# Larger rows for the loads around the layer changes of a two-layer attention and mixer kernel, and weights loaded for two heads at a time

## The chip, the cores and the metric

The kernel runs on one core of one Trainium2 chip. The metric is the device time of one execution in microseconds (us). Three runs of the kernel before took 2493.18, 2493.18 and 2494.72 us, median 2493.18 us.

## What is computed

Two tokens (batch B = 2, one new position each, D = 512 columns) pass twice through the same pair of blocks, so there are two layers with the same weights and the same key and value caches:

```
x = x + attention(layernorm(x), k_cache, v_cache, wq, wo)
x = x + mixer(layernorm(x), w1, b1, w2, b2)
x = x + attention(layernorm(x), k_cache, v_cache, wq, wo)
x = x + mixer(layernorm(x), w1, b1, w2, b2)
```

The attention has 32 query heads in 8 groups; a group of 4 query heads shares one cache of 32768 keys and values of 128 float32 numbers. One (layer, token, group) is a *unit*: 16 MiB of keys and 16 MiB of values are read, 4 rows of scores come out of the keys, a softmax runs over all 32768 scores, and the values are summed with those weights. There are 2 x 2 x 8 = 32 units. The mixer takes one scalar per column through a small network (1792 hidden numbers shared by all columns) with a gelu. A layer's mixer for one token needs all 8 groups of that token; the next layer's queries for that token need the mixer's result.

## The kernel before, in words

A unit's keys and values are each cut into 8 *chunks* of 4096 columns of 128 partitions (2 MiB, 16 KB in each partition's row). One large SBUF tile, `mem`, holds 13 cells of one chunk each (and a small rest); a cell can also be used as two halves. Loads go out on SyncE (SP) alone, in the order of the program, through `load` (L134 to L137, the issue is L136) and, for the weights of a group, `load_weights` (L113 to L115). An issue waits until TensorE has finished with the cells that it overwrites, and whatever stands behind it on SP waits with it.

For each chunk of keys `k_chunk` (L412) issues 8 products (L422) into a bank of scores, for each chunk of values `v_chunk` (L556) issues 8 products (L567) into `acc`; the trace counts two records for a product. VectorE takes maxima and transposes scores, ScalarE takes exponentials. TensorE works through chunks in one global order, `stream`, sorted by a key per chunk: a unit's values come one unit behind, so that keys of unit n+1 alternate with values of unit n. `at(time, ...)` puts the small work (queries, maxima, exponentials, outputs, mixer) between chunks of this order.

In most units four chunks are loaded at a time: rows of 64 KB, 8 MiB a load, into the two halves of the first eight cells. The order of units is chosen so that heads 5 and 7 of both tokens stand in the middle. Around the *changes* (units N1 = 13 and N2 = 16, in which a token's last group of layer 0 is finished) the mixer has to run before the next layer's queries exist. Therefore the unit after next is taken in between, and chunks of head 7 that layer 1 needs again are kept in SBUF, so that they are not read twice: `KEPT_K` names cells for three chunks of keys, `KEPT` cells for seven chunks of values, one of them in part (5 of its 8 pieces stay). While they stay, few cells are left, and the loads of the units at the changes are small: the values of N1 and N2 come chunk by chunk (2 MiB), the keys and values of the unit after them in halves of a chunk (1 MiB) through four half cells that turn, everything else of these units in single chunks, and the units just before N1 in pairs of chunks. `parts` (L845) says which chunks one load takes, `buffer`, `spread`, `half` and `fit` (L139 to L173) find the cells, `load_k` and `load_v` (L389, L493) issue. A half cell can be loaded again only when TensorE has read the half that lies there.

Weights: `wq` and `wo` of one group are 2 MiB in the array `wqo`, and the 4 cells after the ninth take them in turn, a group each, some ten chunks ahead of their first use.

At a change (`change` in the loop over units) TensorE does this after the last chunk of values but one: `mix_1` (L629, the token's x into `bcast`), the last chunk's products, then in turn with the first half chunks of the next keys the sums of `acc` and their products `out_0` to `out_2` (L535, L607, L240), `take_rows` (L621) and `mix_2` (L653), after which `hidden_sum` runs on ScalarE and VectorE for some ten microseconds.

Of the kernel before, what the change touches and what calls it, by code (L numbers as in the profile page):

```python
# [13 lines left out]
P = 128  # L14
CK = 4096
JT = CK // P
NG = 4
# [7 lines left out]
KEPT_K = {0: 0, 1: 1, 2: 9}  # L25
KEPT = {1: (8, 6), 2: (8, 2), 3: (8, 11), 4: (5, 13), 5: (8, 3), 6: (8, 4), 7: (8, 5)}
# [4 lines left out]
PAIRS = (2, 4, 7)  # L31
EVEN = 6
# [10 lines left out]
def gqa_mixer_kernel(ctx: ExitStack, tc: tile.TileContext, x, kt, v, wqo, cols, out):  # L43
# [23 lines left out]
    R = wqo.shape[2] // (2 * D)  # L67
# [28 lines left out]
    W = wqo.shape[2] // 2  # L96
# [16 lines left out]
    def load_weights(h, cell):  # L113
        home[h] = cell
        nc.sync.dma_start(cells(cell), wqo[h])  # L115
# [23 lines left out]
    def buffer(m, limit, until):  # L139

        ks = range(0, limit - m + 1, m) if limit != EVEN else [k + j for k in PAIRS for j in range(0, 2, m)]
        k = min(ks, key=lambda k: (-room(k, m, until), idle(k, m)) if limit == NCH else idle(k, m))
        assert idle(k, m) <= now[0]
        hold(k, m, until)
        return cells(k, m)
# [8 lines left out]
    def fit(k, m, until):  # L154

        return 0 if until > closed.get(int(k), until) else room(k, m, until)
# [10 lines left out]
    def spread(until, parted=False):  # L167

        k = min((*range(WCELL0 + 1), KEPT[3][1]), key=lambda k: (-fit(k, 1, until), idle(k)))
        if fit(k, 1, until) >= 2 and not parted:  # L170
            hold(k, 1, until)
            return [cells(k)]
        return [half(until - 0.5), half(until)]  # L173
# [215 lines left out]
    def load_k(n, c, m, limit):  # L389
        layer, b, h = unit_of(n)  # L390
        stay = h == keeper and c in KEPT_K
        own = KEPT_K[c] if stay else None
        until = k_done[n, c + m - 1]
        if own is not None:
            if stay and not layer:
                until = k_done[units.index((1, b, h)), c + m - 1]
            hold(own, m, until)
            bufs = [cells(own, m)]
        elif limit == RING:
            bufs = spread(until, n in (N1 + 1, N2 + 1) and c > 1)  # L400
# [89 lines left out]
    def load_v(n, c, m, limit):  # L490
# [6 lines left out]
        at = quads(own) if stay else []  # L497
        if stay:
# [8 lines left out]
        elif limit == RING:  # L507
            bufs = spread(until)
        else:
            bufs = [buffer(m, limit, until)]  # L510
# [45 lines left out]
    def v_chunk(n, c, part):  # L556
# [7 lines left out]
        for q in range(part * NG, min(quads, (part + 1) * NG)):  # L564
# [6 lines left out]
                start=(c == 0 and q < NG),  # L571
# [286 lines left out]
    stream = []  # L858
    for n in range(NU):
        stream += [(n * NCH + c + m - 1, 0, n, c, m, limit) for c, m, limit in parts(n, 0)]  # L860
        for c, m, limit in parts(n, 1):
            if n in (N1, N2):
                key = (n + 1) * NCH + 1 + (c + 1) / (2 * NCH)
            elif n in (N1 + 1, N2 + 1):
                key = (n + 1) * NCH - 0.5 + max(c / (2 * NCH) - 0.5, c - 1)
            else:
                key = (n + 1) * NCH + c + m - 1 + (LAG if N1 < n <= N3 else 0)
# [19 lines left out]
    weight_cell = {h: WCELL0 + h % WCELLS for h in heads}  # L887
    again = dict(zip(passing, (WCELL0 + k for k in (0, 2, 3, 1, 0, 2))))
    mixed = {}
    for n in range(NU):  # L890
# [4 lines left out]
        if n:  # L895
# [14 lines left out]
            if place is S[0]:  # L910
                assert v_done[n - 2, HC - 1] <= q2
        if n and (units[n] == (0, 0, h) or h in passing and units[n] == (1, 0, h)):
            at(kbeg[n] - 10, load_weights, h, (again if layer else weight_cell)[h])
# [14 lines left out]
        else:  # L928
            t1 = max(kend + 2, ahead + (2 if urgent else 4))
            at(kend + 1, max_1, n)  # L930
            at(kend + 2, max_2, n)
            t0 = max(k_done[n, HC - 1], v_done[n - 1, HC - 1] if n else 0)
# [3 lines left out]
            at(kend + 2, exponentials, n, 0)  # L936
# [52 lines left out]
    for n in (N1, N2):  # L989
        for c in KEPT_K:  # L990
            book(KEPT_K[c], 2, k_done[n, c] - 1)
        for c in KEPT:
            book(KEPT[c][1], 2 if KEPT[c][0] > QT else 1, v_done[n, c] - 1)
# [3 lines left out]
    closed[WCELL0], closed[WCELL0 - 1] = kbeg[N2 + 1], kbeg[N3 + 2] - 8  # L997
    closed[6] = closed[7] = kbeg[N3 + 2] - 10
# [9 lines left out]
    for _, is_v, n, c, m, limit in stream:  # L1008
        now[0] = t
        (load_v if is_v else load_k)(n, c, m, limit)  # L1010
        for j in range(m):
            for part in range(SUB):
                (v_chunk if is_v else k_chunk)(n, c + j, part)
                if m == 1 and part == 0:
# [7 lines left out]
def _layout(A_x, A_k_cache, A_v_cache, A_wq, A_wo, B_w1, B_b1, B_w2, B_b2):  # L1022
# [14 lines left out]
    for u, a in enumerate(A_k_cache.reshape(B * HKV, SK, DH)):  # L1037
# [3 lines left out]
    wo = A_wo.reshape(HKV, -1, DH, D).transpose(0, 2, 1, 3)  # L1041
    w2 = B_w2.reshape(P, -1)
# [6 lines left out]
        "wqo": np.concatenate([wq.reshape(HKV, P, -1), wo.reshape(HKV, DH, -1)], axis=2),  # L1049
# [27 lines left out]
```

## Time and profile before

| what | value |
|---|---|
| median of three runs | 2493.18 us (2493.18 to 2494.72) |
| the profiled execution's own time | 2493.41 us |
| its span, first to last instruction | 2491.6 us |
| granted TensorE clock | 0.769 |
| read from HBM | 1061.72 MB |
| loads issued on SP | 234, and one store |

The profile's page names engines PE (products), PEld (their weight loads), DVE, ACT, POOL, SP. `SPq` and `ACTq` are the issuing queues. A row of the timeline gives the start in us from the beginning of the span, the duration, the engine, the line of the kernel, the operation with what it writes and reads, the number of instructions merged into the row, and in brackets how long the engine sat idle before it and what ended that. `PE L422 ... [9.37 <-DMA mem<-in_kt_dram]` means that TensorE waited 9.37 us for a load of keys. A row that begins right behind such a wait therefore tells when a load landed.

### The profile page before, as it was taken

To read this page: it belongs to the slowest core of one execution; us is meant where nothing else is said; L and a number is where in the kernel's file an instruction comes from. 1 tells how busy PE (TensorE), PEld (TensorE's weight loads), DVE (VectorE), ACT (ScalarE), POOL (GpSimd) and SP (SyncE) were. 2 spreads that over 40 slices of the span, in tenths; PEclk is the share of its full clock that TensorE was granted. 3 is DMA by queue.
4 is the path that set the end of the run, shared out by engine and by line. 5 is a ranking of instruction groups with operands and counts; after the bars stand their busy time and mean duration, and the time that the engine had idled before them with its cause. 6 is when DMAs were issued, how large, how long until landed. Compare 5 with 4: busy or idle time off the path is not lost.

```text
span 2491.6 us, 20496 instructions
## 1 busy us (share of the span) xinstructions
PE 1378.2 (55%) x9270; PEld 368.8 (15%) x9270; DVE 240.1 (10%) x632; ACT 187.8 (8%) x554; POOL 4.9 (0%) x17
## 2 busy tenths in 40 slices
PE   4544554655445454666677775464546555455546
PEld 1111111111111111111111111111111111111112
DVE  1000000000000000003113110000000000010002
ACT  0000000000000000002012010000000000011002
POOL 0000000000000000000000000000000000000000
PEclk8677767777777777878798787677777777777778
DMA  9999999999999999999999999999999999999996
GB/s 421 436 429 427 439 433 431 435 435 427 431 435 432 432 428 431 431 426 408 427 427 421 426 429 438 427 436 436 431 431 431 429 431 432 434 432 430 433 436 286
DMA packets 34080, 1063.04 MB, mean 427 GB/s; under 512 B 4037, under 2 KB 4041, under 8 KB 4938
## 3 DMA queue, kind: packets, MB, share of 16 engines
q1 hardware_dynamic: 33704, 1061.70, 99.2%
q8 instruction: 73, 1.20, 0.2%
q14 instruction: 13, 0.11, 0.0%
q10 hardware_dynamic: 290, 0.04, 0.0%
HBM read 1061.72 MB, written 0.00 MB: 426 GB/s over the span
## 4 chain that ended last, share of the span: by engine, by line
DMA 75%; PE 24%; issue 0%; DVE 0%; ACT 0%; SPq 0%; POOL 0%
DMA mem<-in_kt_dram 38%; DMA mem<-in_v_dram 37%; PE scores L422 11%; PE acc L567 10%; PE kept L334 1%; PE rows L240 0%; PE bcast L334 0%; PE small L607 0%; PE small L451 0%; PE small L598 0%; PE kept L749 0%; PE small L445 0%; PE bcast L817 0%; ACT S L462 0%; SPq L136 0%
## 5 line engine op out<-in xcount | busy, mean ns | idle before, releaser
L422 PE MATMUL scores<-mem,small_sb 128*32 128x512 f32 x4096 | 629.4, 732 | 608.7 <-DMA mem<-in_kt_dram 608.4
L567 PE MATMUL acc<-mem,S 128*16 128x512 f32 x4088 | 613.3, 736 | 460.3 <-DMA mem<-in_v_dram 457.9
L422 PEld LDWEIGHTS scores<-mem,small_sb 128*32 128x32 f32 x4096 | 147.8, 128 | 1001.0 <-issue 898.8
L462 ACT ACTIVATE S<-S,small_sb 128x128 f32<-128x128 f32 x240 | 123.5, 518 | 2104.4 <-DVE small_sb L453 1630.4
L567 PEld LDWEIGHTS acc<-mem,S 128*16 128x16 f32 x4088 | 133.2, 110 | 823.5 <-issue 674.7
L437 DVE TENSOR_REDUCE small_sb<-scores 128x1 f32<-128x512 f32 x64 | 44.2, 690 | 831.4 <-PE scores L422 831.4
L457 DVE STREAM_TRANSPOSE S<-scores 128x512 f32<-128x512 f32 x64 | 45.4, 710 | 124.0 <-PE acc L567 124.0
L334 PE MATMUL kept<-mem,small_sb 128*2 128x512 f32 x104 | 51.2, 619 | 1.7 <-DVE small_sb L268 1.7
L240 PE MATMUL rows<-mem,small_sb 128*1 128x512 f32 (+1 forms) x276 | 47.1, 601 | 2.6 <-ACT mem L792 2.4
L462 ACT ACTIVATION_READ_ACCUMULATOR S<-S,small_sb 128x1 f32 x240 | 44.8, 187 | 0.0
L447 DVE TENSOR_REDUCE small_sb<-small 1x4 f32<-1x128 f32 x32 | 8.9, 279 | 276.5 <-PE small L445 276.5
L600 DVE RECIPROCAL small_sb<-small 128x4 f32<-128x4 f32 x32 | 5.9, 184 | 291.4 <-PE small L598 291.4
L609 DVE TENSOR_TENSOR small_sb<-small,small_sb 128x4 f32<-128x4 f32 x31 | 5.1, 164 | 291.6 <-PE small L607 291.6
L537 DVE SCALAR_TENSOR_TENSOR S<-acc,small_sb,S 128x128 f32<-128x128 f32 x93 | 32.6, 351 | 3.3
L792 ACT ACTIVATE S<-bcast,small_sb 128x512 f32<-128x512 f32 x28 | 21.6, 777 | 92.4 <-DVE small_sb L661 90.3
L535 DVE TENSOR_SCALAR S<-acc,small_sb 128x128 f32<-128x128 f32 x31 | 10.8, 349 | 158.9 <-PE acc L567 158.9
L360 PE MATMUL small<-small_sb,mem 2*128 2x2 f32 x112 | 14.7, 249 | 17.9 <-DVE mem L356 17.9
L607 PEld LDWEIGHTS small<-small_sb,S 128*128 128x128 f32 x62 | 13.0, 262 | 46.0 <-issue 40.0
L334 PE MATMUL bcast<-mem,small_sb 128*1 128x512 f32 (+1 forms) x40 | 19.1, 592 | 0.0
L809 DVE SCALAR_TENSOR_TENSOR acc<-S,small_sb,acc 128x512 f32<-128x512 f32 x24 | 18.1, 755 | 2.5
L360 PEld LDWEIGHTS small<-small_sb,mem 2*128 2x128 f32 x112 | 13.5, 186 | 30.5 <-DVE mem L356 27.3
L607 PE MATMUL small<-small_sb,S 128*128 128x4 f32 x62 | 15.7, 323 | 1.7 <-DVE S L537 1.7
(134 smaller groups left out, 265.5 us busy)
## 6 DMA issues: line engine op xcount, KB each, us to landing
mem<-in_kt_dram SPq DMA_DIRECT2D x32, 2048.0 KB, 16.5
mem<-in_v_dram SPq DMA_DIRECT2D x23, 2048.0 KB, 20.9
mem<-in_v_dram SPq DMA_DIRECT2D x9, 4096.0 KB, 27.1
mem<-in_wqo_dram SPq DMA_DIRECT2D x14, 2048.0 KB, 33.5
mem<-in_kt_dram SPq DMA_DIRECT2D x7, 4096.0 KB, 23.7
mem<-in_kt_dram SPq DMA_DIRECT2D x24, 1024.0 KB, 8.8
mem<-in_v_dram SPq DMA_DIRECT2D x21, 1024.0 KB, 8.4
mem<-in_v_dram SPq DMA_DIRECT2D x2, 1280.0 KB, 26.5
```

The source lines that it names most:

```text
L240: nc.tensor.matmul(rows[32 * g : 32 * g + b + 1, :], weights if b else weights[:, 1:], row, start=False, stop=True, skip_group_check=True,)
L334: nc.tensor.matmul(q_ps[n][:m, :], xnT[:, d, b : b + m], wq_at(h)[:, d, :], start=(d == 0), stop=(d == DT - 1),)
L360: nc.tensor.matmul(pt[:, r * m : (r + 1) * m], q_row[n][:m, r * DH : (r + 1) * DH], ident[:m, :m], start=True, stop=True,)
L422: nc.tensor.matmul(sc_ps[n, half][32 * g : 32 * g + 32, :], q, kc[k * NG + g], start=(i == 0 and k == 0), stop=(i == PACK - 1 and k == SUB ...
L437: nc.vector.tensor_reduce(mx[n][:, half : half + 1], sc_ps[n, half], axis=AX.X, op=ALU.max)
L457: nc.vector.transpose(S[half], sc_ps[n, half])
L462: nc.scalar.activation(s[:, :, h], s[:, :, h], AF.Exp, bias=neg[n][:, h : h + 1], scale=SCALE, accum_out=lsum[n][:, half, h : h + 1],)
L537: nc.vector.scalar_tensor_tensor(t, acc[:, k * DH : (k + 1) * DH], mask[:, k : k + 1], t, op0=ALU.mult, op1=ALU.add)
L567: nc.tensor.matmul(acc[32 * g : 32 * g + R * QT, :], S[half][:, col : col + R * QT], vc[q], start=(c == 0 and q < NG), stop=(c == NCH - 1 ...
L607: nc.tensor.matmul(po[:, :R], row_tile()[:, :DH], selh, start=True, stop=True)
L792: nc.scalar.activation(hid[key, f], px[key], AF.Gelu_apprx_tanh, bias=shift[key][:, f : f + 1], scale=slope[key][:, f : f + 1],)
L809: nc.vector.scalar_tensor_tensor(h if f == FT - 1 else acc, h, w, acc, op0=ALU.mult, op1=ALU.add)
```

## The change

- The weights of two groups are put into one row of `wqo` on the host (`TWO_HEADS`: groups 0 and 1, 2 and 3, 4 and 6, 5 and 7) and come with one load of 4 MiB (32 KB rows) into two of the four weight cells. There are 7 such loads in place of 14 of 2 MiB.
- The three kept chunks of keys lie in cells 0, 1, 2, the kept whole chunks of values 1, 2, 3 in cells 8, 9, 10 and 5, 6, 7 in cells 3, 4, 5, so that three chunks lie side by side. Keys 0 to 2 and values 1 to 3 and 5 to 7 of N1 and of N2 come in one load of 6 MiB each (48 KB rows).
- The other loads around them take pairs of chunks (32 KB rows) where most were single: keys 4 to 7 of N1 and N2, keys 4 to 7 of N1+2 and N3, values 6 and 7 of N1+1 and N2+1, keys 0 and 1 of N1+1 and N2+1, and all keys of the neighbours on both sides.
- `spread` looks among 11 cells (`RING_CELLS`) and can be told the cell (`PLACE_K`, `PLACE_V`); the values of N1+2 follow an order given by hand (`FOLLOWS`).
- In the units from N1+1 to N3 the maxima and the first exponentials stand up to two chunks earlier in the order; the queries of N3+2 and the weights that they need are asked for later than the others' (4 and 7 chunks ahead).
- The loads of half a chunk at the changes (1 MiB, 45 of them) stay 45, with the cells that turn being 6 and 7 in place of 7 and 8.

No product and no operation of VectorE or ScalarE is added or removed: the built program has 4635 products in both versions. The core of the diff:

```
-KEPT_K = {0: 0, 1: 1, 2: 9}
-KEPT = {1: (8, 6), 2: (8, 2), 3: (8, 11), 4: (5, 13), 5: (8, 3), 6: (8, 4), 7: (8, 5)}
+KEPT_K = {0: 0, 1: 1, 2: 2}
+KEPT = {1: (8, 8), 2: (8, 9), 3: (8, 10), 4: (5, 13), 5: (8, 3), 6: (8, 4), 7: (8, 5)}
+RING_CELLS = 11
+PLACE_K, PLACE_V = {3: 1, 4: 6, 6: 6}, {5: 2, 6: 0}
-PAIRS = (2, 4, 7)
-EVEN = 6
+TWO_HEADS = ((0, 1), (2, 3), (4, 6), RESIDENT)
+FOLLOWS = (2.2, -0.9, -0.8, -0.7, 3.5, 3.6, 3.7, 5.5)
...
-    def load_weights(h, cell):
-        home[h] = cell
-        nc.sync.dma_start(cells(cell), wqo[h])
+    def load_weights(k, cell):
+        for j in range(2):
+            home[TWO_HEADS[k][j]] = cell + j
+        nc.sync.dma_start(cells(cell, 2), wqo[k])
...
+        if stay and m > 1:
+            k = KEPT[c][1]
+            own = cells(k, m)
+            load(own, src)
...
-        if m == N1:
-            loads = ((0, 2), (2, 2), (4, 2), (6, 2)) if with_v else ((0, 2), (2, 1), (3, 1), (4, 2), (6, 2))
-            return [(c, k, EVEN) for c, k in loads]
-        return [(c, 1, EVEN if n == N1 + 1 and not with_v and c < 2 else RING) for c in range(NCH)]
+        if not with_v:
+            loads = ((0, 3), (3, 1), (4, 2), (6, 2)) if n in (N1, N2) else ((0, 2), (2, 2), (4, 2), (6, 2))
+            if n in (N1 + 1, N2 + 1):
+                loads = ((0, 2), *((c, 1) for c in range(2, NCH)))
+            if n in (N1 + 2, N3):
+                loads = (*((c, 1) for c in range(4)), (4, 2), (6, 2))
+        elif n in (N1, N2):
+            loads = ((0, 1), (1, 3), (4, 1), (5, 3))
+        elif n in (N1 + 1, N2 + 1):
+            loads = (*((c, 1) for c in range(6)), (6, 2))
+        elif n < N1:
+            loads = ((0, 2), (2, 2), (4, 2), (6, 2))
+        else:
+            loads = [(c, 1) for c in range(NCH)]
+        return [(c, k, RING) for c, k in loads]
...
-            q0 = kbeg[n] - (10 if n == N3 + 1 else 6)
+            q0 = kbeg[n] - (10 if n == N3 + 1 else 4 if n == N3 + 2 else 6)
...
-            at(kbeg[n] - 10, load_weights, h, (again if layer else weight_cell)[h])
+            at(kbeg[n] - (7 if n == N3 + 2 else 10), load_weights, opens[h], WCELL0 + opens[h] % 2 * 2)
...
-            at(kend + 1, max_1, n)
-            at(kend + 2, max_2, n)
+            e = kend if N1 < n <= N3 else kend + 2
+            at(max(kend, e - 1), max_1, n)
+            at(e, max_2, n)
...
-        "wqo": np.concatenate([wq.reshape(HKV, P, -1), wo.reshape(HKV, DH, -1)], axis=2),
+        "wqo": np.stack([np.concatenate([wqo[h] for h in two], axis=1) for two in TWO_HEADS]),
```

In the built program SP issues 202 loads in place of 234. By size (row of one partition): 64 KB 95 in both; 48 KB 0 before and 6 after; 32 KB 16 and 36; 16 KB 69 and 11; 8 KB 45 in both; the other nine (0.25 to 1.25 MiB) are the same. Lines move by 3 to 11: L136 becomes L139, L115 becomes L118, L422 becomes L425, L567 becomes L578.

More of the change, by code (lines that the diff above doesn't have):

```diff
@@ L66, in gqa_mixer_kernel @@
     HKV = U // B
-    R = wqo.shape[2] // (2 * D)
+    R = wqo.shape[2] // (4 * D)
     DT = D // P
@@ L139, in buffer @@
     def buffer(m, limit, until):
-        ks = range(0, limit - m + 1, m) if limit != EVEN else [k + j for k in PAIRS for j in range(0, 2, m)]
-        k = min(ks, key=lambda k: (-room(k, m, until), idle(k, m)) if limit == NCH else idle(k, m))
+        k = min(range(0, limit - m + 1, m), key=lambda k: (-room(k, m, until), idle(k, m)))
         assert idle(k, m) <= now[0]
@@ L154, in fit @@
     def fit(k, m, until):
-        return 0 if until > closed.get(int(k), until) else room(k, m, until)
+        shut = any(until > closed.get(j, until) for j in range(int(k), int(-(-(k + m) // 1))))
+        return 0 if shut else room(k, m, until)
     def room(k, m, until):
@@ L165, in between, with spread @@
         return sum(brings[int(-(-a // 1)) : b])
[L167 to L172, printed above, removed]
+    def spread(m, until, parted=False, place=None):
+        ks = range(RING_CELLS - m + 1) if place is None else [place]
+        k = min(ks, key=lambda k: (-fit(k, m, until), idle(k, m)))
+        if fit(k, m, until) >= 2 and not parted:
+            hold(k, m, until)
+            return [cells(k, m)]
+        assert m == 1
         return [half(until - 0.5), half(until)]
@@ L391, in load_k @@
         stay = h == keeper and c in KEPT_K
-        own = KEPT_K[c] if stay else None
         until = k_done[n, c + m - 1]
[L394 to L398, printed above, removed]
+        if stay:
+            for j in range(m):
+                hold(KEPT_K[c + j], 1, k_done[units.index((1, b, h)), c + j])
+            bufs = [cells(KEPT_K[c], m)]
         elif limit == RING:
-            bufs = spread(until, n in (N1 + 1, N2 + 1) and c > 1)
+            bufs = spread(m, until, n in (N1 + 1, N2 + 1) and m == 1, PLACE_K.get(c) if n in (N1 + 2, N3) else None)
         else:
```

47 lines of the change are left out of this document (28 added, 19 removed).

## Prediction

> **What bounds the kernel now.** I read the page first: the DMA line and its GB/s, the queues, the chain that ended last; then the windows for three stages and the tail, and last the timeline of TensorE, where a load's landing shows as the end of a wait.
>
> ```profile
> PE 1378.2 (55%) x9270; PEld 368.8 (15%) x9270; DVE 240.1 (10%) x632; ACT 187.8 (8%) x554; POOL 4.9 (0%) x17
> DMA  9999999999999999999999999999999999999996
> DMA 75%; PE 24%; issue 0%; DVE 0%; ACT 0%; SPq 0%; POOL 0%
> ```
>
> ```profile
> 0.00:1016.70 1016.70, 514.14 (x3450) 140.80 (x3450) 72.72 (x212) 52.70 (x193) 1.66 (x11) 0.75 1.00 431
> 1016.70:1487.40 470.70, 324.97 (x2092) 78.55 (x2092) 83.62 (x187) 54.64 (x130) 2.17 (x4) 0.83 1.01 424
> 1487.40:2475.20 987.80, 527.45 (x3552) 142.32 (x3552) 74.68 (x210) 72.88 (x223) 0.54 (x1) 0.76 1.00 430
> 2475.20:2491.60 16.40, 11.60 (x176) 7.11 (x176) 9.12 (x24) 7.58 (x8) 0.54 (x1) 1.00 0.01 2
> ```
>
> The DMA engines are busy from the first to the last load, and TensorE, the busiest engine, has 55%. The last three numbers of a window are the granted clock, the DMA share and GB/s. The middle window holds the units at the changes: it runs at 424 GB/s where the others have 431 and 430, and its DMA share is still 1.01. So the queue does not starve there; the small loads only carry fewer bytes per time. The time is therefore the sum of the loads' own times plus a tail of 16.4 us in which nothing is loaded. If the whole middle ran at 431, it would be 470.7 x (1 - 424/431) = 7.6 us shorter. That is an upper bound of what larger rows can give.
>
> **What a load costs by its size.** The ends of TensorE's waits give the spacing of landings:
>
> ```profile
> 490.83 6.11 PE L567 MATMUL acc<-mem,S 128*16 128x512 f32 x32 [9.09 <-DMA mem<-in_v_dram]
> ...
> 510.18 8.42 PE L422 MATMUL scores<-mem,small_sb 128*32 128x512 f32 x64 [9.37 <-DMA mem<-in_kt_dram]
> 529.53 3.62 PE L567 MATMUL acc<-mem,S 128*16 128x512 f32 x16 [10.92 <-DMA mem<-in_v_dram]
> ```
>
> ```profile
> 1536.32 5.32 PE L567 MATMUL acc<-mem,S 128*16 128x512 f32 x32 [4.38 <-DMA mem<-in_v_dram]
> 1545.94 5.93 PE L422 MATMUL scores<-mem,small_sb 128*32 128x512 f32 x32 [4.30 <-DMA mem<-in_kt_dram]
> 1555.64 2.76 PE L567 MATMUL acc<-mem,S 128*16 128x512 f32 x12 [3.77 <-DMA mem<-in_v_dram]
> ```
>
> ```profile
> 1133.77 3.26 PE L567 MATMUL acc<-mem,S 128*16 128x512 f32 x16 [3.86 <-DMA mem<-in_v_dram]
> 1138.66 1.91 PE L567 MATMUL acc<-mem,S 128*16 128x512 f32 x16 [1.63 <-DMA mem<-in_v_dram]
> 1140.50 1.16 PE L629 MATMUL bcast<-small_sb 128*128 128x128 f32 x8
> 1143.57 1.91 PE L567 MATMUL acc<-mem,S 128*16 128x512 f32 x16 [1.91 <-DMA mem<-in_v_dram]
> 1146.06 1.06 PE L422 MATMUL scores<-mem,small_sb 128*32 128x512 f32 x8 [0.58 <-DMA mem<-in_kt_dram]
> 1147.11 0.39 PE L607 MATMUL small<-small_sb,S 128*128 128x4 f32 x2
> 1148.55 1.06 PE L422 MATMUL scores<-mem,small_sb 128*32 128x512 f32 x8 [1.05 <-DMA mem<-in_kt_dram]
> 1149.43 1.04 PE L240 MATMUL rows<-mem,small_sb 128*1 128x512 f32 x8
> 1151.29 1.12 PE L653 MATMUL bcast<-S,small_sb 128*128 128x512 f32 x2 [0.81 <-DVE S L621]
> 1152.34 2.23 PE L422 MATMUL scores<-mem,small_sb 128*32 128x512 f32 x16
> ```
>
> 8 MiB take 19.35 us (510.18 to 529.53), 4 MiB (1555.64 - 1536.32)/2 = 9.66, 2 MiB (1143.57 - 1133.77)/2 = 4.90, 1 MiB 2.49. Four loads of 2 MiB cost 19.60, one of 8 MiB 19.35: 0.25 us for three loads more, 0.08 each. Eight of 1 MiB cost 19.92: 0.57 for seven, 0.08 each. So a queued load has its bytes' time and about 0.075 us of its own; 0.05 to 0.10 are the ends that single spacings allow.
>
> The Trainium skill, DMA: Bandwidth & Descriptors, section "Anatomy of one DMA", puts a fixed part of about 2.0 us on each DMA beside its bytes. By that, the 32 loads saved would be worth about 64 us, an estimate; the spacing of 2.49 us for 1 MiB has no room for it, so queued loads here overlap it.
>
> **The change part by part.**
>
> *Fewer loads.* These rows of the DMA issues are the ones that change:
>
> ```profile
> mem<-in_kt_dram SPq DMA_DIRECT2D x32, 2048.0 KB, 16.5
> mem<-in_v_dram SPq DMA_DIRECT2D x23, 2048.0 KB, 20.9
> mem<-in_v_dram SPq DMA_DIRECT2D x9, 4096.0 KB, 27.1
> mem<-in_wqo_dram SPq DMA_DIRECT2D x14, 2048.0 KB, 33.5
> mem<-in_kt_dram SPq DMA_DIRECT2D x7, 4096.0 KB, 23.7
> ```
>
> 69 loads of 2 MiB and 16 of 4 MiB (202 MiB) become 11 of 2, 36 of 4 and 6 of 6 MiB (202 MiB). Bytes stay; 32 loads go: 32 x 0.075 = **-2.4 us** (1.6 to 3.2). A 48 KB row is in no row here; it lies between 32 and 64 KB, whose times are proportional, so I cost it by bytes.
>
> *Weights in pairs.* The first load is 4 MiB in place of 2, so the first keys land 4.9 us later, and the weights of group 1 are not loaded later: no change of the sum.
>
> ```profile
> 28.28 2.78 PE L422 MATMUL scores<-mem,small_sb 128*32 128x512 f32 x11 [7.44 <-DMA mem<-in_kt_dram]
> ```
>
> The queries are ready 7.44 us before the first keys; weights and keys both move by 4.9, so the cover stays. Cost nothing. If that cover were gone, the third load of keys would still have the time of a whole load (19.35) queued ahead of it. Later pairs are asked for early (median 33.5 us to landing) except one, below.
>
> *Order of small work.* Maxima, exponentials and queries move by one to four chunks; counts stay. VectorE and ScalarE are busy 83.62 and 54.64 of 470.70 us in the middle. They matter only through cells that come free late, which is the next term.
>
> *Cells that come free later.* A load of three chunks lands at once, after 14.5 us in which TensorE has little to do. At a change, values 5 to 7 land together, at L, say. Behind them stand four half chunks of keys in cells that are already free, so the queue has work until their last landing at L + 4 x 2.48 = L + 9.9. The fifth half overwrites the first, so SP holds it until TensorE has done, in the built order: chunks 5 and 6, `mix_1`, chunk 7, the first half of keys. By the rows of 1133 to 1147: 3.5 for a chunk after a wait (3.26 there, up to 3.62 at 529.53), 1.8 for one right behind another, 1.0 (L629 overlaps), 1.8 and 1.1: 9.2 us. In the kernel before only chunk 7 was left when the last load of values landed, so the same half was free at 1147.1 while halves were landing until 1146.06 + 3 x 2.48 = 1153.5: over 6 us of cover. That cover is used up.
>
> What is late next depends on how long an issue takes to become a landing with an idle queue, F beside the bytes' time. Nothing shows an idle queue in mid-run. The two nearest rows: weights at the very start, 7.9 us for 2 MiB, so 3.0; and the load issued at 1180.72, used at 1186.22, 2.59 after the one before it (so the queue lost 0.1 at most): 5.5 - 2.5 = 3.0 or less.
>
> ```profile
> DMA to landing us min/median/max: 7.9/33.5/36.7
> ```
>
> ```profile
> 1180.72 0.33 SPq L136 DMA_DIRECT2D mem<-in_v_dram  x1
> ```
>
> ```profile
> 1183.63 1.05 PE L567 MATMUL acc<-mem,S 128*16 128x512 f32 x8 [0.15 <-DMA mem<-in_v_dram]
> ...
> 1186.22 1.04 PE L567 MATMUL acc<-mem,S 128*16 128x512 f32 x8
> ```
>
> F lies between 0 and 3.0; I take 1.5, the middle. Then the fifth half lands (9.2 + 1.5) - 9.9 = 0.8 us late (0 to 2.3). The seventh waits for a second thing: between the second and third half stand L607, L240, VectorE's L621, L653, from 1149.43 to about 1153.5, 4.1 us. It is issued at about L + 9.2 + 0.4 + 0.9 + 4.1 = L + 14.6, lands with F 16.1 + 2.5, and the sixth landed at L + 9.9 + 0.8 + 5.0 = L + 15.7: 0.4 late (0 to 0.7). Queued behind each waiting issue on SP are only the next halves, which need later reads anyway. Two changes: 2 x 1.2 = **+2.4 us** (0 to 6.0).
>
> One pair of weights (groups 0 and 1, layer 1) overwrites the cells of kept values 2 and 3 and now waits for TensorE:
>
> ```profile
> 1435.43 0.44 SPq L115 DMA_DIRECT2D mem<-in_wqo_dram  x1
> ```
>
> ```profile
> 1452.56 1.93 PE L422 MATMUL scores<-mem,small_sb 128*32 128x512 f32 x16 [0.56 <-DMA mem<-in_kt_dram]
> 1454.30 1.90 PE L567 MATMUL acc<-mem,S 128*16 128x512 f32 x16
> ```
>
> Before, it went out without waiting, with three more loads queued ahead of it. After, a pair of keys lands, then two chunks of keys (3.5 + 1.8) and two of kept values (1.8 + 1.8), 8.9 us, then the issue; one pair of keys (9.7) covers it. 8.9 + 1.5 - 9.7 = **+0.7 us** (0 to 2.2). Queued behind it on SP are a rest of values and pairs of keys that TensorE needs only after the keys landed by then.
>
> *Sum.* -2.4 + 2.4 + 0.7 = +0.7 us on the profiled execution's own 2493.41 (span 2491.6; it is 0.2 above the median): 2494.1, rounded to **2494 us**. About 0.2% (5 us, 2488.2 to 2498.2) is what a measurement of this kernel can tell from no change.
>
> **Rivals.**
> 1. *No late cell at all.* If F is near 0 or TensorE is some tenths quicker, only the saving is left: 2493.4 - 2.4 = 2491.0. For it: the queue has run without a gap on leads as short as at 1180.72. Against it: the working above. Still within 0.2%.
> 2. *TensorE stays slow through the joined chunks (slower).* The first 16 records after a wait take 3.26, later ones 1.91. Halves at 1146.06 and 1148.55 take 1.06, but others take longer:
>
> ```profile
> 1158.43 1.94 PE L422 MATMUL scores<-mem,small_sb 128*32 128x512 f32 x8 [1.30 <-DMA mem<-in_kt_dram]
> 1160.92 1.94 PE L422 MATMUL scores<-mem,small_sb 128*32 128x512 f32 x8 [0.55 <-DMA mem<-in_kt_dram]
> ```
>
>    If all three chunks run at 3.5, each change is 2 x 1.7 = 3.4 us later, and the weights' wait 3 x 1.7 = 5.1: +11.9, 2506. It passes 2498.2 when about a third of that comes true. Against it: 32 records in a row took 5.32 at 1536.32, 3.4 + 1.9. The Trainium skill, TensorE: Matmul & The Clock Gate, Part 1, says that the first 3.4 us or so after an idle window run at half clock. The trace agrees (3.26 against 1.91 for 16 records), and it speaks against joining chunks, since it makes waits longer; by it alone the slow part is paid once per landing, as I did.
> 3. *The middle reaches the rate of the rest (faster).* -7.6, 2485.8. For it: 69 loads of 2 MiB are nearly gone. Against: the 45 loads of 1 MiB stay, and the price per load is the same by two ways. A fixed part of 3.0 us that isn't overlapped would give 32 x 3.0 = 96, 2397; the spacing of 2.49 excludes it. By the 2.0 us of the Trainium skill (DMA: Bandwidth & Descriptors, "Anatomy of one DMA") it would be 2429, an estimate that the same spacing excludes.
> 4. *The change doesn't do what it says.* The built program's loads have the sizes counted above; no chance.
>
> **How the numbers follow.** Forecast (late cells, 2492 to 2498) 0.58; rival 1 0.28; rival 2 beyond 2498.2 0.09; rival 3 0.04, a fixed part 0.01. Range: 2490.5 (the saving at its middle, no late cell, less a half for the run) to 2498.5 (bounds 6.0 + 2.2 less the saving: 2499.2, cut, since both ends would have to come together). Faster by over 0.2%: 0.05; within: 0.86; slower: 0.09.
>
> **What would show it.** Loads of 6 MiB spaced by 14.5 us; the middle about 2 us shorter in DMA time; at both changes the fifth half's issue 9 to 10 us behind TensorE's first product on value chunk 5, and there a spacing of landings of 3.3 in place of 2.49; DMA share dipping there alone; the tail still 16.4 us. Wrong if gaps stand elsewhere, if the second and third joined chunk take over 3 us, or if a 48 KB row costs more than its bytes.

## The result, and the profile after

The changed kernel takes 2503.58 us (median of 6 runs, 2502.12 to 2507.31), the kernel before 2493.45 us on the same chip: ratio 1.0043, 95% interval 1.0030 to 1.0056. It is slower by about 10 us, where 0.7 was forecast, and above the range of 2490.5 to 2498.5. The profiled execution took 2506.48 us (span 2504.7), 2.9 above the median; this matters below.

Four rows of the changed kernel's page: the engines' busy time, GB/s in 40 slices (62.6 us each), the instruction fetches, and the chain that ended last.

```profile
PE 1371.3 (55%) x9270; PEld 372.4 (15%) x9270; DVE 240.2 (10%) x632; ACT 187.8 (7%) x554; POOL 4.9 (0%) x17
...
GB/s 419 434 434 429 439 433 433 430 433 435 434 434 431 432 432 434 424 432 378 425 428 395 399 409 432 435 434 433 433 431 431 435 434 433 435 430 435 430 431 284
...
q8 instruction: 73, 1.20, 0.2%
...
DMA 73%; PE 25%; issue 0%; DVE 0%; another core or an unknown queue 0%; ACT 0%; SPq 0%
```

Work and bound are the same. Between 1127 and 1503 us four slices fall to 378 to 409 GB/s. The windows of that stretch, of the changed kernel and then of the kernel before (the last two numbers of a row are the DMA share and GB/s):

```profile
1010.00:1140.00 130.00, 72.76 (x472) 18.89 (x472) 10.93 (x32) 10.12 (x34) 0.00 (x0) 0.76 1.00 430
1140.00:1180.00 40.00, 29.55 (x180) 7.37 (x180) 18.84 (x37) 12.87 (x17) 1.09 (x2) 0.80 0.90 365
1180.00:1340.00 160.00, 103.23 (x714) 26.78 (x716) 19.20 (x45) 11.05 (x36) 0.00 (x0) 0.82 1.00 423
1340.00:1380.00 40.00, 31.80 (x206) 8.68 (x202) 22.67 (x44) 14.13 (x19) 1.08 (x2) 0.91 0.92 373
1380.00:1425.00 45.00, 27.93 (x186) 6.98 (x178) 3.81 (x8) 0.00 (x0) 0.00 (x0) 0.85 0.99 411
1425.00:1490.00 65.00, 41.32 (x272) 10.78 (x274) 6.41 (x16) 4.17 (x16) 0.00 (x0) 0.77 0.95 395
```

```profile
1010.00:1140.00 130.00, 79.01 (x504) 19.77 (x504) 10.72 (x32) 10.21 (x34) 0.00 (x0) 0.79 1.00 425
1140.00:1180.00 40.00, 28.89 (x166) 6.73 (x162) 19.86 (x40) 13.49 (x18) 1.09 (x2) 0.87 1.00 407
...
1340.00:1380.00 40.00, 30.07 (x190) 7.43 (x194) 22.59 (x42) 14.13 (x19) 1.08 (x2) 0.91 1.01 418
...
1425.00:1490.00 65.00, 48.26 (x342) 13.15 (x338) 8.71 (x25) 6.29 (x24) 0.00 (x0) 0.85 1.01 429
```

Up to 1140 us the larger rows do what they should: 430 GB/s in place of 425. At the two changes and at the weights the DMA share falls to 0.90, 0.92 and 0.95, where before it was 1.00 to 1.01: 40 x 0.10 + 40 x 0.09 + 65 x 0.06 = 11.5 us without bytes. The tail is 16.45 us (16.4 before):

```profile
2488.25:2504.70 16.45, 11.60 (x176) 7.11 (x176) 9.13 (x24) 7.57 (x8) 0.54 (x1) 0.98 0.01 2
```

**Late landings.** The trace records when each load has landed, with sixteen completions per load, of which the last is the landing. Call *late* what lies between two landings beyond the time of the bytes (2.41 us per MiB and 0.066 per load: 2.48 us for 1 MiB, 4.89, 9.71, 14.5 and 19.35 for 2, 4, 6 and 8). A 6 MiB load between two landings of the changed kernel took 1256.69 - 1242.15 = 14.54 us: rows of 48 KB cost their bytes. Summed by place, in us, for one profile of each kernel (for the changed kernel three, of its first run and of two of the runs below):

| kernel | first change (1145 to 1171) | second change (1340 to 1372) | the pair of weights | all other | last landing |
|---|---|---|---|---|---|
| before | 0.4 | 0.1 | 0.0 | 14.9 | 2475.20 |
| changed, first profile | 3.7 | 4.4 | 3.0 | 20.2 | 2488.25 |
| changed, second (e8) | 3.8 | 4.6 | 3.3 | 15.6 | 2484.56 |
| changed, third (e10) | 4.6 | 3.7 | 2.7 | 15.3 | 2483.65 |
| e1, last value chunk alone | 0.3 | 0.2 | 4.4 | 15.0 | 2477.43 |
| e2, last two joined | 3.4 | 2.6 | 4.2 | 15.1 | 2482.99 |
| e3, weights behind keys | 4.8 | 4.8 | 0.0 | 18.4 | 2485.23 |
| e11, the same again | 5.2 | 4.0 | 0.0 | 14.9 | 2481.39 |
| e4, named chunks alone | 4.8 | 4.0 | 3.7 | 13.0 | 2483.05 |
| e6, changes and weights | 0.1 | 0.2 | 0.0 | 16.1 | 2474.05 |
| e5, all three | 1.0 | 0.1 | 0.0 | 15.8 | 2474.56 |
| e9, before with the last three joined | 4.3 | 4.5 | -0.1 | 16.7 | 2485.03 |

The saving is there: in the three profiles of the changed kernel the late landings grow by 15.7, 11.9 and 10.8 us and the last landing moves by 13.05, 9.36 and 8.45, which leaves 2.4 to 2.6 us for the 32 loads fewer. This is no second measurement of what a load costs: 32 x 0.066 = 2.1 of it is the price per load by which *late* is counted. The first profile has 5 us at other places that the later two do not have.

**How a gap looks.** TensorE at the first change of the changed kernel, and SP's issue of the fifth half of keys:

```profile
1142.47 5.14 PE L578 MATMUL acc<-mem,S 128*16 128x512 f32 x32 [9.39 <-DMA mem<-in_v_dram]
1147.53 1.16 PE L640 MATMUL bcast<-small_sb 128*128 128x128 f32 x8
1148.62 1.91 PE L578 MATMUL acc<-mem,S 128*16 128x512 f32 x16
1150.35 1.04 PE L425 MATMUL scores<-mem,small_sb 128*32 128x512 f32 x8
```

```profile
1151.45 0.33 SPq L139 DMA_DIRECT2D mem<-in_kt_dram  x1
```

The joined values land at L = 1142.42, TensorE goes through the order that the prediction names, and the issue comes at L + 9.0 (9.2 worked out). The last free half lands at 1152.30, L + 9.9, as worked out. But not all of the queue worked until then. DMA share ahead of, up to and behind that landing, and below it the row of the kernel before that ends with its last free half (1153.46):

```profile
1144.00:1147.00 3.00, 3.00 (x24) 0.66 (x20) 0.00 (x0) 0.00 (x0) 0.00 (x0) 0.74 0.97 401
1147.00:1152.30 5.30, 4.52 (x42) 1.73 (x34) 1.41 (x4) 0.00 (x0) 0.00 (x0) 1.00 0.42 173
1152.30:1154.00 1.70, 1.70 (x18) 0.53 (x18) 0.17 (x1) 0.00 (x0) 0.00 (x0) 1.00 0.92 270
```

```profile
1147.00:1153.50 6.50, 4.54 (x32) 1.12 (x29) 2.56 (x8) 0.00 (x0) 0.00 (x0) 1.00 1.00 391
```

For 5.3 us ahead of the last queued landing the share is 0.42, so on average more than half of the DMA engines have nothing left: 5.3 x 0.58 = 3.1 us of the engines' time, *before* the moment from which the prediction began to count. Whether this idle time makes a later load late is a question of its own, and the sums under e8 answer it. In the kernel before the next half had been issued at 1147.19, and the share stays 1.00. The fifth half of the changed kernel lands at 1156.12, 4.67 us behind its issue and 2.2 beside its bytes (the last number of its row among the DMA issues):

```profile
mem<-in_kt_dram SPq DMA_DIRECT2D x1, 1024.0 KB, 4.7
```

The Trainium skill, DMA: Bandwidth & Descriptors, section "Why a DMA increments its semaphore by 16 and not by 1", says that a DMA runs on up to 16 engines that finish independently, and that its count is full only when the last has finished. The trace agrees: the sixteen completions of the last free half run from 1147.21 to 1152.30, 5.1 us apart, and half of them come before 1147.8. Those of the fifth half, behind the hole, lie 0.5 us apart.

### The profile page after: what moved, and what is told of

It reads as the page before. It is cut to its first block, busy times and chain, and to the rows that moved or that the text cites. A ratio compares the mean times of both kernels' runs of the same rounds, so it can differ in the third digit from the quotient of the medians.

```text
span 2504.7 us, 20445 instructions
## 1 busy us (share of the span) xinstructions
PE 1371.3 (55%) x9270; PEld 372.4 (15%) x9270; DVE 240.2 (10%) x632; ACT 187.8 (7%) x554; POOL 4.9 (0%) x17
## 4 chain that ended last, share of the span: by engine, by line
DMA 73%; PE 25%; issue 0%; DVE 0%; another core or an unknown queue 0%; ACT 0%; SPq 0%
DMA mem<-in_v_dram 65%; PE acc L578 20%; DMA mem<-in_kt_dram 9%; PE scores L425 4%; PE bcast L339 0%; PE small L454 0%; PE small L609 0%; PE small L448 0%; PE rows L245 0%; PE kept L760 0%; PE small L618 0%; PE bcast L664 0%; PE bcast L640 0%; DVE S L548 0%
## 5 line engine op out<-in xcount | busy, mean ns | idle before, releaser
L425 PE MATMUL scores<-mem,small_sb 128*32 128x512 f32 x4096 | 632.7, 737 | 610.7 <-DMA mem<-in_kt_dram 610.5
L578 PE MATMUL acc<-mem,S 128*16 128x512 f32 x4088 | 602.1, 727 | 469.7 <-DMA mem<-in_v_dram 467.3
L425 PEld LDWEIGHTS scores<-mem,small_sb 128*32 128x32 f32 x4096 | 150.4, 129 | 996.9 <-issue 904.8
L578 PEld LDWEIGHTS acc<-mem,S 128*16 128x16 f32 x4088 | 134.5, 110 | 829.8 <-issue 669.9
L546 DVE TENSOR_SCALAR S<-acc,small_sb 128x128 f32<-128x128 f32 x31 | 10.8, 350 | 177.8 <-PE acc L578 177.8
L365 PEld LDWEIGHTS small<-small_sb,mem 2*128 2x128 f32 x112 | 13.5, 186 | 32.1 <-DVE mem L361 29.7
L448 PE MATMUL small<-small_sb 128*1 128x128 f32 x64 | 17.1, 361 | 0.6 <-DVE small_sb L446 0.3
## 6 DMA issues: line engine op xcount, KB each, us to landing
mem<-in_kt_dram SPq DMA_DIRECT2D x2, 6144.0 KB, 22.1
```

Source lines behind the costliest of these rows:

```text
L365: nc.tensor.matmul(pt[:, r * m : (r + 1) * m], q_row[n][:m, r * DH : (r + 1) * DH], ident[:m, :m], start=True, stop=True,)
L425: nc.tensor.matmul(sc_ps[n, half][32 * g : 32 * g + 32, :], q, kc[k * NG + g], start=(i == 0 and k == 0), stop=(i == PACK - 1 and k == SUB ...
L448: nc.tensor.matmul(pm[:1, :P], mxa, ident, start=True, stop=True)
L578: nc.tensor.matmul(acc[32 * g : 32 * g + R * QT, :], S[half][:, col : col + R * QT], vc[q], start=(c == (n == N1 + 2) and q < NG), stop=(c ...
```

## The experiments

The theories: **A**, late cells as in the prediction, under-priced because the DMA engines run dry one by one; rivals **B** (large rows cost more than their bytes), **C** (TensorE is slow over joined chunks) and **D** (later gaps are after-effects of the earlier ones). Theory A has a rival that keeps its late cells: a *flat* time of about 2.2 us from issue to landing beside the bytes, which has to be covered up to the last queued landing, whatever the engines that finish earlier do. The expectations of e2 and e7 name it. All kernels are the changed one with the edit shown, except e7 and e9, which start from the kernel before.

**e1.** The last value chunk alone at both changes.

```
-            loads = ((0, 1), (1, 3), (4, 1), (5, 3))
+            loads = ((0, 1), (1, 3), (4, 1), (5, 2), (7, 1))
```

> The changed kernel, but at both changes the last value chunk is a load of its own (chunks 5 and 6 together, 7 alone). Theory A (the 16 DMA engines drain the queue each for itself and up to some us apart, so a load has to be issued about 3 us, for pairs about 5 us, before the last landing of what is queued): the gaps at the two changes go, 3.7 and 4.2 us of late landings; those at about 1242, 1407 to 1448 and 1485 us stay; two loads more cost 0.15. 2503.6 - 7.9 + 0.15 = 2495.8, between 2494 and 2498. Theory B (rows of 48 KB or larger loads cost more than their bytes): only two of six such loads go, so a third of the 10 us, 2500. Theory C (TensorE runs the joined chunks slowly and frees the cells late): one chunk in three is out of the way, 2 to 4 us, 2500 to 2502. Theory D (the later gaps are only after-effects of those at the changes): all go, 2489 to 2491.

Measured 2496.95 us (11 runs, 2495.28 to 2500.28), 1.0014 (1.0005 to 1.0023) of the kernel before. The gaps at the changes are gone (0.3 and 0.2), the one at the weights stays: so far as theory A and as a flat time have it, and against B and D. The later gaps that the expectation left standing are gone too (15.0 at all other places); most of them stood in the changed kernel's first profile only, as e8 and e10 show. The fifth half is issued 4.8 us ahead of the last queued landing. The DMA share still dips there (this row; the rows around it have 0.95 and 1.01),

```profile
1147.00:1149.90 2.90, 2.12 (x22) 0.66 (x18) 1.48 (x5) 0.00 (x0) 0.00 (x0) 1.00 0.73 277
```

so even with 4.8 us of cover some engines wait (the completions ahead of it lie 5.9 us apart), but not the slowest, and no landing is late. A dip of the share ahead of a landing is by itself no loss.

**e2.** Chunk 5 alone, 6 and 7 joined.

```
-            loads = ((0, 1), (1, 3), (4, 1), (5, 3))
+            loads = ((0, 1), (1, 3), (4, 1), (5, 1), (6, 2))
```

> The changed kernel, but at both changes value chunk 5 is alone and 6 and 7 come together. The fifth half of keys is then issued at about L + 3.5 + 1.0 + 1.8 + 1.1 = L + 7.4, 2.5 us before the last landing of what is queued (L + 9.9). By the prediction on record (1.5 us from issue to landing beside the bytes' time) that is cover enough: no gap at the changes, the same time as with the last value chunk alone. Theory A: 2.5 us of cover are too few, since in the changed kernel halves issued 2.52 and 2.55 us ahead landed 0.49 and 0.91 us late: 0.5 to 1.5 us stay late at each change, 2496.5 to 2499. A flat 2.2 us from issue to landing, with no engines apart: 0 late, 2495.8.

Measured 2501.1 us (7 runs), 1.0030 (1.0018 to 1.0041): more than any of the theories gave. TensorE needed 8.5 us in place of 7.4 (its first chunk 3.62 and `mix_1`, which now fell into its slow stretch, 2.08 in place of 1.0), so that the halves went out only 1.1 to 1.9 us ahead; they were 0.2 to 0.9 late, and two fetches came on top. So this run shows part of theory C, and not what 2.5 us of cover would do. Lead and lateness of these four halves add up to 2.0 to 2.1 us (1.42 + 0.69, 1.12 + 0.93, 1.94 + 0.18, 1.13 + 0.87), as with a flat time.

**e3 and e11.** The one pair of weights behind one more pair of keys, its queries two chunks later.

```
-                q0 = kbeg[n] - (10 if n == N3 + 1 else 4 if n == N3 + 2 else 6)
+                q0 = kbeg[n] - (10 if n == N3 + 1 else 2 if n == N3 + 2 else 6)
...
-            at(kbeg[n] - (7 if n == N3 + 2 else 10), load_weights, opens[h], WCELL0 + opens[h] % 2 * 2)
+            at(kbeg[n] - (3 if n == N3 + 2 else 10), load_weights, opens[h], WCELL0 + opens[h] % 2 * 2)
```

> The changed kernel, but the pair of weights of groups 0 and 1 for layer 1 is asked for behind one more pair of keys, and its queries are made two chunks later. Theory A: the 2.95 us by which that pair landed late go and nothing else changes: 2503.6 - 3.0 = 2500.6. Theory D (it is an after-effect of the gaps ahead of it): no change, 2503.6. By the prediction on record 0.7 us go, 2502.9; the landing of this pair in the trace tells these apart, since the time alone does so hardly.

Measured 2502.96 us (6 runs, 2499.23 to 2503.47). The time alone hardly moved, though the weights' gap was gone; in that profile both changes were at 4.8. The second comparison stands beside the changed kernel on one chip:

> The changed kernel with the one pair of weights behind one more pair of keys, timed beside the changed kernel on one chip, since the first comparison (2502.96 against 2503.58) was made in six runs each that lie 4 us apart. On top of the first edit (last value alone) the same edit took 3.8 us off. If the weights' gap is a loss of its own: 3 us below the changed kernel. If it only takes over what other gaps leave: within 1 us of it.

> The changed kernel again, on the same chip as the next one: 2503 to 2504, and a third profile. Its fifth half of keys at a change is issued 9.0 to 10.3 us behind the joined landing.

Measured 2502.03 us (9 runs) against 2505.88 for the changed kernel (5 runs, 2501.96 to 2507.68): 3.9 below, in few runs that lie 6 to 7 us apart. With e3 the two comparisons give 0.6 and 3.9. That the gap is a loss of its own rests on the landings (0.0 at the weights in e3 and e11, nothing added elsewhere in e11) and on e6, which has the same edit on top of e1 and is 3.8 us below it (3.5 by the ratios, since the two ran on two chips). In the changed kernel's first profile the pair is issued 0.84 us ahead of the last queued landing (1472.66); the first row is the issue, the second the window up to that landing:

```profile
1471.82 0.33 SPq L118 DMA_DIRECT2D mem<-in_wqo_dram  x1
```

```profile
1467.00:1472.70 5.70, 4.75 (x48) 0.98 (x36) 1.56 (x3) 0.00 (x0) 0.00 (x0) 1.00 0.51 218
```

It is the same picture, and the pair lands 2.95 late, 13.5 us behind its issue:

```profile
mem<-in_wqo_dram SPq DMA_DIRECT2D x1, 4096.0 KB, 13.5
```

Fifteen of its sixteen completions come 1.3 to 1.9 us ahead of the last one, and a fetch of 0.9 us runs at 1477.3, while it loads.

**e4.** Key chunks 4 to 7 of N1+2 and N3 and value chunks 6 and 7 of N1+1 and N2+1 alone.

```
-PLACE_K, PLACE_V = {3: 1, 4: 6, 6: 6}, {5: 2, 6: 0}
+PLACE_K, PLACE_V = {3: 1, 4: 6, 5: 7, 6: 6, 7: 7}, {}
...
-                loads = (*((c, 1) for c in range(4)), (4, 2), (6, 2))
+                loads = (*((c, 1) for c in range(4)), (4, 1), (5, 1), (6, 1), (7, 1))
...
-            loads = (*((c, 1) for c in range(6)), (6, 2))
+            loads = [(c, 1) for c in range(NCH)]
```

> The changed kernel, but behind the changes key chunks 4 to 7 of the one unit and value chunks 6 and 7 of the other are loads of their own again, in the same or other free cells: six loads more, 0.4 us. The gaps at the changes and at the weights stay as they are. Theory A: the late landings at about 1242 (1.1), 1407 (1.1) and 1448 us (2.6), where pairs were issued only 3.0 to 3.6 us ahead, go: 2503.6 - 4.8 + 0.4 = 2499.2. Theory D (those come from engines that the gaps at the changes have levelled): they stay somewhere, 2503 to 2504. Theory B (larger loads cost more): 2501 to 2502.

Measured 2501.95 us (6 runs), 1.0031 (1.0019 to 1.0043). The late landings behind the changes go (13.0 at other places, the least of all), but the time falls by 1.6 us against 2503.58 and not by 4.4: the 5 us at these places stood in the first profile only, as e8 shows. The expectation was wrong, because it took one execution for the rule.

**e5 and e6.** e6 has the edits of e1 and e3. e5 has besides, of e4, keys 4 and 5 and values 6 and 7 alone:

```
-PLACE_K, PLACE_V = {3: 1, 4: 6, 6: 6}, {5: 2, 6: 0}
+PLACE_K, PLACE_V = {3: 1, 6: 6}, {5: 2}
...
+                loads = (*((c, 1) for c in range(4)), (4, 1), (5, 1), (6, 2))
...
+            loads = [(c, 1) for c in range(NCH)]
```

> The changed kernel with two edits: last value chunk alone at the changes, and weights behind one more pair of keys. The named pairs behind the changes stay, with their loads issued 3.0 to 3.6 us ahead. With the last value alone these pairs were 0.3 to 0.8 us late at a place, in the changed kernel 1.1 to 2.6. If they cost what they cost in the changed kernel (4.8): 2491.5 + 4.8 = 2496; if short cover hurts only where a gap shortly before has levelled the engines (part of theory D): about 2 us late in all, 2493 to 2494.

> The changed kernel with three edits together: last value chunk alone at the changes, weights behind one more pair of keys, and behind the changes key chunks 4 and 5 and value chunks 6 and 7 alone (keys 6 and 7 stay a pair). 209 loads, 26 fewer than before, four of them with rows of 48 KB. If late landings are the whole loss (theory A, whatever the cause of each), only the saving of the loads is left: 26 x 0.075 = 2.0, 2493.6 - 2.0 = 2491.6, with some tenths for what the last value alone left late (0.2 to 0.8 at a place): 2491.5 to 2493. Theory B (48 KB rows or larger loads cost more): four of six stay, 2497 to 2500.

e6 measured 2493.14 us (11 runs, 1.0000, 0.9991 to 1.0009), e5 2492.32 (11 runs, 0.9995, 0.9986 to 1.0004), the kernel before beside them 2493.42. Two edits take back the whole loss, although four 48 KB loads and nearly all pairs stay: theory B falls. The expectation of e6 asked besides whether short cover hurts more behind a gap. That stays undecided: without the gaps those pairs went out 4.3 to 5.2 us ahead, where the changed kernel's had 3.0 to 3.7. The windows of e5:

```profile
1140.00:1180.00 40.00, 32.11 (x194) 7.62 (x186) 20.35 (x40) 13.48 (x18) 1.09 (x2) 0.84 0.99 398
...
1340.00:1380.00 40.00, 30.49 (x198) 7.55 (x202) 21.92 (x41) 14.11 (x19) 1.08 (x2) 0.91 1.01 417
...
1425.00:1490.00 65.00, 46.86 (x304) 11.92 (x305) 6.13 (x15) 4.15 (x16) 0.00 (x0) 0.78 1.00 425
```

The share is back at 0.99 to 1.01. That 26 loads fewer make e5 faster than the kernel before (1.1 us by the medians, 2.0 expected) is inside the interval and not shown.

**e7.** Known gaps in a steady stretch of the kernel before: four 8 MiB loads of keys go into the cells of the values just ahead of them.

```
+        if m == 4 and now[0] in (64, 96, 128, 160):
+            k = max(ks, key=lambda k: idle(k, m))
```

> The kernel before, with four loads of keys of 8 MiB in a steady stretch (about 335, 505, 675 and 845 us) each put into the cells of the values just ahead of it, so that each waits for TensorE's products on these (10.4 us) with an empty queue. The time of one such gap is 10.4 and what lies between issue and landing beside the bytes' time. Flat 2.1 us, as for the half chunks of the changed kernel: issue to landing 21.4 us, 4 x 12.5 = 50, 2543.5. If what lies there grows with the load (3.9 for the 4 MiB of weights): issue to landing 23.2 or more, 4 x 14.3 = 57, 2550. On top, if a gap levels the engines so that the next instruction fetch's 1 us reaches the landings instead of being hidden: 1 us for each gap, 4 more.

Measured 2546.6 us (4 runs), 53.2 above the kernel before: between the two sums. Two of the four issues, and the first products on what they brought:

```profile
338.73 0.33 SPq L136 DMA_DIRECT2D mem<-in_kt_dram  x1
```

```profile
360.82 10.03 PE L424 MATMUL scores<-mem,small_sb 128*32 128x512 f32 x64 [22.15 <-DMA mem<-in_kt_dram]
```

```profile
512.45 0.33 SPq L136 DMA_DIRECT2D mem<-in_kt_dram  x1
```

```profile
534.57 8.50 PE L424 MATMUL scores<-mem,small_sb 128*32 128x512 f32 x64 [22.18 <-DMA mem<-in_kt_dram]
```

From issue to use 22.1 us (to the recorded landing, 534.43, 22.0), of which 19.35 are bytes: 2.6 to landing on an empty queue. So it is 2.0 to 2.2 for 1 MiB and little more for 8 (2.4 to 2.6 at the four gaps). The four loads themselves are 49.1 us late together, all landings 66.9, and 17.8 are left for the others (15.4 before). Behind each gap, where the completions of a load lie 0.5 to 0.8 us apart, the next fetch shows at once with a landing 1.1 us late (at 400.7, 554.9, 728.3 and 921.5); but some of the late landings of the kernel before (350, 652, 934) do not come, and what is left is 2.4 us for four gaps. Theory D is worth little.

**e8.** The changed kernel again, unedited, for its profile.

> The changed kernel once more, for a second profile: how much the late landings at each place differ between two executions of one kernel. The two records of value chunks 5 and 6 after the joined landing took 5.14 and 5.94 us in the first profile, 6.4 to 6.5 in two of its variants. If TensorE's slow stretch varies, the fifth half is issued 9.0 to 10.3 us behind the landing and lands 1.3 to 2.6 us late; the sum of issue lead and lateness stays at 2.0 to 2.2 for halves and 3.8 to 4.0 for the pair of weights.

2502.77 us. The first record behind the joined landing, in e8, e10 and e11 (in the first profile 5.14):

```profile
1142.59 5.26 PE L578 MATMUL acc<-mem,S 128*16 128x512 f32 x32 [9.27 <-DMA mem<-in_v_dram]
```

```profile
1142.69 6.25 PE L578 MATMUL acc<-mem,S 128*16 128x512 f32 x32 [9.99 <-DMA mem<-in_v_dram]
```

```profile
1142.43 6.58 PE L578 MATMUL acc<-mem,S 128*16 128x512 f32 x32 [9.65 <-DMA mem<-in_v_dram]
```

The same 32 records take 5.14 to 6.58 us, and the fifth half is issued L + 9.0 to L + 10.5. This is what varies from run to run. How long ahead of the last queued landing it goes out, plus how late it lands, is nearly constant: 0.85 + 1.35, 0.73 + 1.50, -0.25 + 2.28 at the first change, 0.26 + 1.97, -0.16 + 2.27, 0.74 + 1.27 at the second, 2.0 to 2.2 as expected; for the weights 0.84 + 2.95, 0.50 + 3.33, 0.96 + 2.69, and -0.40 + 4.35 in e1: 3.7 to 4.0.

These sums also tell theory A from the flat time. Ahead of the fifth half the completions lay 5.1 to 6.1 us apart at the first change and 2.3 to 2.9 at the second, and the sum is the same. At the seventh halves, behind the gap, they lay 0.5 to 1.2 us apart, and those that went out less than 2.2 us ahead give 1.69 + 0.73, 2.14 + 0.20, 1.53 + 0.62, 1.05 + 1.02 and 1.41 + 0.71: again 2.1 to 2.4. If early engines made a load late, the sum would have to grow with their distance, and it does not. So the late cells and the wait for TensorE of theory A stand, and its second half, the engines that run dry one by one, falls: a half is late by what its lead to the *last* queued landing lacks of 2.0 to 2.2 us.

**e9.** The kernel before with one part of the change: value chunks 5 to 7 joined at both changes.

```
+        if stay and m > 1:
+            k = KEPT[c][1]
+            load(cells(k, m), src)
+            for j in range(m):
+                hold(k + j, 1, v_done[units.index((1, b, h)), c + j])
+                v_at[n, c + j] = quads(cells(k + j))
+            return
...
+        if with_v and n in (N1, N2):
+            return [(c, 1, RING) for c in range(5)] + [(5, 3, RING)]
...
-                if m == 1 and part == 0:
+                if part == 0:
```

> The kernel before with one part of the change alone: at both changes value chunks 5 to 7 come as one load of 6 MiB into the cells in which they are kept (4 loads fewer, -0.3); everything else is as before. By the steps on record, 1.2 us late at a change: 2493.5 + 2.4 - 0.3 = 2495.6. Theory A with what the two profiles of the changed kernel show at the changes (3.7 and 4.2, 3.8 and 4.6 us of late landings, an instruction fetch's 1.1 at each among them): 2493.5 + 8.1 - 0.3 = 2501.3; without the fetches, since the kernel before has some of those at other places, 2499. If the gaps need the other parts of the change as well, 2493 to 2495.

Measured 2501.74 us (7 runs), 1.0029 (1.0018 to 1.0040): 7.3 above, where the steps on record give 2.1. One load in place of three, twice, is most of the loss without any other part of the change. Its last free half lands at 1153.37, the fifth is issued at 1153.23 and lands 1.87 late: 0.14 + 1.87 = 2.0 once more. The window around this landing has the same hole:

```profile
1148.00:1154.20 6.20, 5.43 (x46) 1.96 (x38) 1.40 (x4) 0.00 (x0) 0.00 (x0) 0.99 0.41 166
```

## Why the prediction was wrong

- *Fewer loads, -2.4*: nothing speaks against it (2.4 to 2.6 are left by the landings), but no run shows it by its time: e6 with 30 loads fewer and e5 with 26 lie inside the interval of the kernel before. Weights in pairs at the start and the order of the small work, 0: right as far as the windows show (1.00 and 430 GB/s up to 1140 us).
- *Cells that come free later, +2.4 (0 to 6.0)*: **the step that failed, in its size.** Place, order and mechanism were right: L + 9.0 to 10.1 in the three profiles against 9.2 for the issue, L + 9.9 for the cover, and a load that is late by what the cover lacks. Measured are 3.7 to 4.6 us at each change in place of 1.2. The fifth half is 1.3 to 2.3 late in place of 0.8: F is 2.0 to 2.2 in place of 1.5 (inside its bounds), and TensorE's path is up to 0.9 longer than worked out (1.3 in e11). The halves behind it were together 1.0 to 1.9 late, in place of 0.4. At five of the six changes another 1.1 to 1.3 came where an instruction fetch fell behind the gap; that part was not in the sum at all. Some of it only comes earlier than it would have (e7). The sentence that "the queue has work until their last landing" does not hold for most of the engines, which stood idle for up to 5 us ahead of it; but the landings do not follow from that (e1, e8).
- *The pair of weights, +0.7 (0 to 2.2)*: right place, wrong size: 2.7 to 3.3, and up to 4.4. The wait, from 1462.97 to 1471.82, was the 8.9 us worked out (10.1 in e1), but issue to landing beside the bytes is 3.7 to 4.0 in place of 1.5. In each of these profiles a fetch of 0.9 to 1 us fell into that load, and one of its sixteen completions came 1.2 to 1.5 us behind the other fifteen. Without that one 2.3 to 2.6 are left, as for the loads of e7. That the late engine is the one with the fetch fits, but the trace does not name a fetch's engine.
- *Sum*: -2.5 + 8.2 + 3.0 = +8.7, and up to 5 us at other places in single runs; measured +10.
- *Rival 1* (no late cell) and *rival 3* fall. *Rival 2* gave about the right time, 2506, for a reason that is the smaller part: TensorE's slow stretch lasts longer in some runs (6.58 for what took 5.14), but only one pair of chunks is hit, 0 to 1.3 us at a change.
- *"Gaps there alone"* was wrong: halves and pairs that went out 2.3 to 4.5 us ahead were late at times (0.01 to 2.3 us), where in the kernel before a half issued 2.9 us ahead was not late.

The Trainium skill, DMA: Bandwidth & Descriptors, section "Anatomy of one DMA", gives about 2.0 us as the fixed part of one DMA, for DMAs issued from GpSimd (SWDGE). Spacings in a full queue do not show it, and so the prediction set it aside; the 2.0 to 2.2 us that the loads issued on SP take here on an empty queue are near it.

What stays open: why some loads with more than 2.2 us of cover were late all the same. Of the halves issued 2.3 to 2.9 us ahead several landed in time to 0.05 us; others were up to 1.15 late, with one to three of their sixteen completions behind the rest and no fetch recorded there.

## What to carry to other kernels

When the DMA queue is the bound, issue a load ahead of the last landing of what is queued by the time that it takes from issue to landing on an empty queue beside its bytes: 2.0 to 2.2 us for 1 MiB here, 2.4 to 2.6 for 8 MiB, and 1.1 to 1.5 more where an instruction fetch falls behind a gap. Spacings in a full queue do not show this time, and a DMA share that dips ahead of a landing is by itself no loss. A larger load makes everything behind its landing bunch up: three chunks that land at once cost 0.3 us less in loads and 7 us in cells that came free late. One profile shows where the gaps are; how large they usually are takes two or three.

## What the runs showed of the hardware

- On an empty queue a load lands 2.0 to 2.2 us (1 MiB) or 2.4 to 2.6 us (8 MiB, e7) later than its bytes take; in a full queue it costs 0.07 us beside them.
- The same 32 records (16 products) behind a wait of 9 to 10 us took 5.14 to 6.58 us in different runs; in the first profile the granted clock was 0.74 from 1144 to 1147 us and 1.00 behind it. The Trainium skill, TensorE: Matmul & The Clock Gate, Part 1, says that the gate watches a free-running window and that the slow stretch varies from run to run; these rows agree.
- In the steady stretches of the kernel before, landings jump by 1.2 to 1.6 us at 68, 350, 652 and 934 us and again at 1697, 1985 and 2281, every 280 to 300 us, each time with an instruction fetch (16 KB, 1 us on one engine) during the loads concerned; the other fetches there do not show. Meanwhile the sixteen completions of one load move apart: 1.0 us at 47, 2.2 at 68, 3.6 at 350, 5.1 at 652 and 5.9 at 934. So there is room to hide a fetch in engines that are ahead of the slowest. A gap takes this room away: behind it the completions lie 0.5 to 0.8 us apart, and the next fetch shows with 1.1 us behind each of the four gaps of e7.
